# Three loads and one DMA transpose moved to other places in their queues, in a block-sparse attention with a residual MLP behind it

## The chip, the cores and the metric

The kernel runs on one core of a Trainium2 chip. The metric is the device time of one execution in microseconds (us). A core has TensorE (PE in the profile, its weight loads PEld), VectorE (DVE), ScalarE (ACT), GpSimd (POOL) and SyncE (SP). Each takes its instructions in order. Loads and stores are carried by 16 DMA engines; an instruction on POOL or SP only issues them.

## The reference

Block-sparse attention over 4 batches, 8 heads, 768 positions and 64 values per head, followed by a residual MLP with a mixing step over positions. In short:

```python
scores = (1 / sqrt(D)) * q @ k.T           # per batch and head
mask   = window | first/last block row and column | 3 sampled blocks per block row
attn   = softmax(where(mask, scores, -1e9))
x      = (attn @ v)  as [batch, seq, heads * D]       # d_model 512
a1  = alpha1 * x + beta1
tok = einsum('ts,bsd->btd', w_tok, a1)
u   = x + lam * tok
a2  = alpha2 * u + beta2
out = u + lam * (relu(a2 @ w_ch1) @ w_ch2)            # w_ch1 512 x 2048
```

## The kernel before, in words

Work goes by pairs of heads: pair i holds heads 2(i mod 4) and 2(i mod 4)+1 of batch i // 4, so there are 16 pairs, 0 to 15, four for each batch. For a pair, q, k and v are loaded with a cast to 16 bits (L322, issued on POOL), q and k are transposed, scores are computed on TensorE (L605), exponentiated on ScalarE (L623), multiplied with v on TensorE (L652 for early pairs, L675 for late ones), and normalised on VectorE (L692, L693). Behind it come the affine step (L709, L710, on POOL or VectorE), the mixing over positions (L826, L850), a cast (L869), a transpose of u (by TensorE, or by DMA on SP's queue at L902) with an affine step behind it (L893), and the two matmuls of the MLP (L923, L1075), which are woven into the attention of the next batch. Stores are issued on SP (L1088).

Two written lists set the order of the work around the change.

`PLAN` covers pairs 0 to 4, which run in 45 slots. It gives each side job a number: the whole part is the slot, the rest orders jobs within the slot (under 0.5 in the slot's early half). `loadq4` is the load of pair 4's q; `tq4`, `tk4` are pair 4's transposes on TensorE (L515), `tq5`, `tk5` those of pair 5 (L555); `lv4`, `lv5` copy v into place on VectorE (L333); `mask..` are copies on POOL (L541), `w1_..`, `w2_..` loads of the MLP's weights (L775, L781). The numbers are no times: a job runs when its engine comes to it.

`W1`, `W2`, `W2L` and `W3` cover the rest. Each row is a third of a pair, each letter a step: `d` issues one DMA transpose of u (L902), `v` the affine step on its result (L893), `g` four matmuls of the second MLP layer and after every fourth `g` a store, `K` and `Q` the DMA transposes of the next pair's k (L566) and q (L571, L574). Rows 1 and 2 of `W2L` belong to pair 12; the transposes there are those of pairs 10 and 11, the last of batch 2 counted from 0.

Buffers set what a load must wait for: q has two buffers (`qpad`), k and v have two each (`kr`, `vr`). Pair 4's loads overwrite pair 2's data, so they wait for pair 2's transposes on TensorE, and pair 5's for pair 3's.

```python
def emit_load(i, which="qkv"):                    # line 311
    ...
        nc.gpsimd.dma_start(                      # line 322
            t, src[b, 2 * hp : 2 * hp + 2].rearrange("w (p o) d -> p w (o d)", o=NT)
        )
...
def fns(s, late):                                 # line 1416
    for when, name in sorted(slots.get(s, ())):
        if (when % 1 >= 0.5) == late:
            jobs_of[name]()
```

Of the kernel before, what the change touches and what calls it, by code (L numbers as in the profile page):

```python
# [66 lines left out]
]  # L67
W2L = [
# [91 lines left out]
    "tok0_1": 16.29,  # L160
    "tok0_2": 17.09,
    "tok0_3": 18.68,
    "loadq4": 18.7,
    "lv3": 19.01,
    "loadk4": 19.19,
    "tok0_4": 19.61,
    "mask5": 20.08,
    "mask9": 20.29,
    "tq3": 20.7,
    "tok0_5": 20.76,  # L170
    "loadv5": 20.77,
    "loadq5": 21.09,
    "tk3": 22.44,
    "loadk5": 22.78,
    "udma0": 23.28,
# [1394 lines left out]
```

## Time and profile before

| | |
|---|---|
| median of 3 runs | 297.3 us (297.27 to 297.41) |
| the profiled execution | 297.57 us |
| its span, first to last instruction | 295.9 us |
| granted TensorE clock | 1.0 throughout |
| bytes moved by DMA | 31.09 MB, 105 GB/s on average |

A line of a timeline gives the start and the length of a group of like instructions in us, the engine, the line of the kernel, the operation, out<-in by the program's names, the shapes and the count; in brackets stands the idle time just before it and what ended that. A line of DMA issues gives out<-in, the issuing queue, the count, KB each (of what is written), and the us from issue to landing. In the chain of work that ended last, a line is start, length, and what.

### The profile page before, as it was taken

To read this page: it belongs to the slowest core of one execution; us is meant where nothing else is said; L and a number is where in the kernel's file an instruction comes from. 1 tells how busy PE (TensorE), PEld (TensorE's weight loads), DVE (VectorE), ACT (ScalarE), POOL (GpSimd) and SP (SyncE) were. 2 spreads that over 40 slices of the span, in tenths; PEclk is the share of its full clock that TensorE was granted. 3 is DMA by queue.
4 is the path that set the end of the run, shared out by engine and by line. 5 is a ranking of instruction groups with operands and counts; after the bars stand their busy time and mean duration, and the time that the engine had idled before them with its cause. 6 is when DMAs were issued, how large, how long until landed. Compare 5 with 4: busy or idle time off the path is not lost.

```text
span 295.9 us, 7583 instructions
## 1 busy us (share of the span) xinstructions
PE 289.2 (98%) x3097; PEld 192.7 (65%) x3097; DVE 240.6 (81%) x498; ACT 217.0 (73%) x324; POOL 110.1 (37%) x149
## 2 busy tenths in 40 slices
PE   7999999999999999999999999999999999999995
PEld 2678878665467565565576556465567678766884
DVE  4988899995668887988758788795946999999894
ACT  5999989999799872999779780899869764477000
POOL 8997978632343720347321450335320300000000
PEclk9999999999999999999999999999999999999999
DMA  6999999981392996737962957653520214400023
GB/s 176 204 198 167 193 158 204 177 143 27 95 143 60 106 190 103 109 75 98 122 122 57 142 77 161 91 123 44 96 62 2 53 38 20 151 1 3 0 91 124
DMA packets 57274, 31.09 MB, mean 105 GB/s; under 512 B 37204, under 2 KB 54016, under 8 KB 57240
## 3 DMA queue, kind: packets, MB, share of 16 engines
q0 software_dynamic: 16752, 14.22, 33.6%
q1 hardware_dynamic: 40020, 15.92, 28.2%
q8 instruction: 24, 0.39, 0.6%
q10 hardware_dynamic: 468, 0.47, 0.6%
q14 instruction: 10, 0.08, 0.1%
HBM read 29.75 MB, written 6.29 MB: 122 GB/s over the span
## 4 chain that ended last, share of the span: by engine, by line
PE 84%; DVE 5%; ACT 4%; DMA 4%; issue 1%; POOL 1%; POOLq 0%
PE mm L923 20%; PE mm L1075 16%; PE sp L605 8%; PE op L675 8%; PE mm L850 8%; PE mm L1189 5%; ACT eT L623 4%; PE mm L605 3%; DMA kr<-in_k_dram 3%; PE sp L1189 3%; PE sp L1036 3%; PE mm L1036 3%; PE op L652 2%; PE mm L826 2%; DVE eT L640 1%; DMA x_sb<-in_q_dram 1%
## 5 line engine op out<-in xcount | busy, mean ns | idle before, releaser
L623 ACT ACTIVATE eT<-sp,expb 128x1024 f16<-128x1024 f32 x111 | 118.4, 1118 | 2.4 <-PE sp L605 1.8
L640 DVE TENSOR_TENSOR eT<-eT,mask 128x1024 f16<-128x1024 f16 x99 | 80.1, 835 | 14.2 <-ACT eT L623 14.0
L709 POOL TENSOR_TENSOR a1pp<-x_sb,vbc 128x384 bf16<-128x384 f32 x25 | 28.5, 1139 | 119.2 <-DVE x_sb L693 84.6
L923 PE MATMUL mm<-uT,w1b 128*128 128x384 bf16 x384 | 70.6, 326 | 0.1
L623 ACT ACTIVATE eT<-mm,expb 128x512 f16<-128x512 f32 x66 | 41.7, 684 | 26.6 <-PE mm L605 26.3
L1075 PE MATMUL mm<-w2b,hts 128*128 128x512 bf16 x224 | 54.7, 380 | 0.0
L930 ACT ACTIVATE hts<-mm 128x384 bf16<-128x384 f32 x96 | 45.1, 501 | 10.1 <-PE mm L923 9.5
L923 PEld LDWEIGHTS <-w1b 128*128 128x128 bf16 x384 | 35.6, 98 | 23.9 <-issue 2.4
L675 PEld LDWEIGHTS <-eT 128*128 128x128 f16 x792 | 29.8, 98 | 8.5 <-issue 1.7
L1075 PEld LDWEIGHTS <-hts 128*128 128x128 bf16 x224 | 19.8, 98 | 22.3 <-issue 3.9
L675 PE MATMUL op<-vext,eT 128*128 128x65 f16 x792 | 32.2, 194 | 0.0
L605 PE MATMUL sp<-qTs,kTs 88*128 88x512 bf16 (+1 forms) x120 | 27.0, 325 | 1.3 <-ACT eT L623 0.7
L710 POOL TENSOR_TENSOR a1pp<-a1pp,vbc 128x384 bf16<-128x384 bf16 x25 | 26.9, 1075 | 2.0
L850 PE MATMUL mm<-a1pp,wtokT 128*128 128x256 bf16 x216 | 25.9, 273 | 0.1
L850 PEld LDWEIGHTS <-wtokT 128*128 128x128 bf16 x216 | 20.6, 98 | 5.6 <-issue 1.8
L1189 PEld LDWEIGHTS <-hts 128*128 128x128 bf16 x208 | 19.6, 98 | 3.3 <-issue 0.3
L862 DVE TENSOR_TENSOR x_sb<-x_sb,mm 128x512 f32<-128x512 f32 x18 | 12.3, 684 | 9.9 <-PE mm L850 9.8
L605 PE MATMUL sp<-qhT,khT 64*128 64x256 bf16 (+1 forms) x176 | 19.8, 322 | 0.0
L605 PEld LDWEIGHTS <-khT 64*128 64x128 bf16 x264 | 10.6, 94 | 12.7 <-issue 9.2
L652 PEld LDWEIGHTS <-eT 128*128 128x128 f16 x360 | 14.9, 98 | 3.8 <-issue 0.3
L1084 DVE TENSOR_TENSOR x_sb<-x_sb,mm 128x512 f32<-128x512 f32 x14 | 9.6, 685 | 8.8 <-PE mm L1075 8.7
L693 DVE TENSOR_TENSOR x_sb<-op,rcp 128x384 f32<-128x384 f32 x28 | 15.6, 557 | 1.0
(137 smaller groups left out, 395.2 us busy)
## 6 DMA issues: line engine op xcount, KB each, us to landing
out_dram<-x_sb SPq DMA_DIRECT2D x23, 256.0 KB
qpad<-in_q_dram POOLq DMA_DIRECT2D x15, 192.0 KB, 4.5
kr<-in_k_dram POOLq DMA_DIRECT2D x15, 192.0 KB, 5.3
vr<-in_v_dram POOLq DMA_DIRECT2D x15, 192.0 KB, 5.9
w1b<-in_moe_w_ch_dram POOLq DMA_DIRECT2D x4, 512.0 KB, 9.8
w2b<-in_moe_w_ch_dram POOLq DMA_DIRECT2D x4, 512.0 KB, 8.5
hts<-in_moe_w_tok_dram POOLq DMA_DIRECT2D x2, 576.0 KB, 8.9
x_sb<-in_k_dram ACTq DMA_DIRECT2D x2, 192.0 KB
```

The source lines that it names most:

```text
L605: nc.tensor.matmul(sp[jj][:, dst], lhsT, rhs, start=True, stop=True, skip_group_check=True,)
L623: nc.scalar.activation(dst, at, AF.Exp, bias=expb[:], scale=SCALE)
L640: nc.vector.tensor_mul(out=e, in0=e, in1=keep)
L652: nc.tensor.matmul(op[0][:, o, :], ets[u][:, jj, h * QB + n * P : h * QB + n * P + P], vexts[i % NVB][:, w, 2 * jp + jj, :], start=op[1] == 0,
L675: nc.tensor.matmul(op[0][:, o, :], ets[u][:, jj, h * QB + n * P : h * QB + n * P + P], vexts[i % NVB][:, w, 2 * jp + jj, :], start=op[1] == 0,
L709: eng.tensor_tensor(out=dst, in0=x_sbs[b][:, :, cols], in1=bc[0], op=ALU.mult)
L710: eng.tensor_tensor(out=dst, in0=dst, in1=bc[1], op=ALU.add)
L850: nc.tensor.matmul(ps[:, o], wtokT[:, os_, ts(2 * n + o, P)], a1pps[i][:, os_, :], start=(os_ == 0 and o == 0), stop=(os_ == NT - 1 and o ...
L923: nc.tensor.matmul(ps[:, 0:QC], w1b[:, dk, ts(n, P)], uTs[b][:, dk, ts(c, QC)], start=(dk == 0), stop=(dk == 3),)
L930: nc.scalar.activation(h_row(b, c, n), ps[:, 0:QC], AF.Relu)
L1075: nc.tensor.matmul(ps[:], ht[:, nk, ts(o % 3, P)], w2b[:, nk, :], start=(nk == 0), stop=(nk == NH - 1),)
L1189: nc.tensor.matmul(ps, a_of(b, t, a)[:, r], b_rows(m, r)[:, 0, cols], start=(start and r == ends[0]), stop=(r == ends[1]), skip_group_chec ...
```

## The change

Four edits. In `PLAN`, pair 4's q is loaded behind `tq2` (15.38), ahead of pair 4's v (15.44), and pair 4's k behind `tk2` (15.49), where both were in slots 18 and 19. Pair 5's q is loaded behind `tq3` (20.7), ahead of pair 5's v (20.77). In `W2L`, the second `d` moves from row 2, where it stood behind a `g`, to stand right behind the first in row 1.

On POOL this gives, in order of issue: the two w2b loads, q4, v4, k4, the affine step L709 and L710, two mask copies, q5, v5, k5. Before it was: the two w2b loads, v4, L709, L710, q4, k4, two mask copies, v5, q5, k5. On SP the order of two instructions changes: the second L902 now comes ahead of one store. TensorE, VectorE and ScalarE have the same instructions in the same order.

```diff
 W2L = [
     "q 0 p p g k x L x p f k 1 K 2 k",
-    "q Q 0 g x g f v v s T T x k 1 k p p g g T g g Y d 2 k",
-    "q g 0 k g d 1 2 p x k g x k",
+    "q Q 0 g x g f v v s T T x k 1 k p p g g T g g Y d d 2 k",
+    "q g 0 k g 1 2 p x k g x k",
...
-    "loadq4": 18.7,
+    "loadq4": 15.391,
     "lv3": 19.01,
-    "loadk4": 19.19,
+    "loadk4": 15.495,
...
     "loadv5": 20.77,
-    "loadq5": 21.09,
+    "loadq5": 20.705,
```

## The prediction

> **What bounds the kernel now.** I read the page first (span and busy shares), then the waits and the chain of work that ended last to find where the moved loads matter, then the timelines of the engines around that place, and last the DMA issues, asked load by load.
>
> ```profile
> span 295.9 us, 7583 instructions
> PE 289.2 (98%) x3097; PEld 192.7 (65%) x3097; DVE 240.6 (81%) x498; ACT 217.0 (73%) x324; POOL 110.1 (37%) x149
> ...
> PEld L515 <- DMA kr<-in_k_dram: 0.6, 1, 0.6
> ...
> 29.05 8.63 DMA kr<-in_k_dram
> ```
>
> TensorE is busy for 289.2 of 295.9 us, so a change can gain only where TensorE stands still or where the engine that feeds it is late. The waits name one such place for the loads that move: the transposes of pair 4's k (L515) waited once for its load. The chain has the same load in it: issued at 29.05, 8.63 us long. Here is POOL, which issues every load, around that time (start, length, engine, line, what):
>
> ```profile
> 15.28 0.76 POOL L775 DMA_DIRECT2D w1b<-in_moe_w_ch_dram  x1
> ...
> 24.07 0.72 POOL L322 DMA_DIRECT2D vr<-in_v_dram  x1
> 26.22 0.99 POOL L709 TENSOR_TENSOR a1pp<-x_sb,vbc 128x384 bf16<-128x384 f32 x1 [1.44 <-DVE x_sb L693]
> 27.29 1.06 POOL L710 TENSOR_TENSOR a1pp<-a1pp,vbc 128x384 bf16<-128x384 bf16 x1
> 28.29 0.76 POOL L322 DMA_DIRECT2D qpad<-in_q_dram  x1
> 29.05 0.72 POOL L322 DMA_DIRECT2D kr<-in_k_dram  x1
> ...
> 30.42 0.72 POOL L322 DMA_DIRECT2D vr<-in_v_dram  x1
> 31.13 0.72 POOL L322 DMA_DIRECT2D qpad<-in_q_dram  x1
> ...
> 37.39 0.99 POOL L709 TENSOR_TENSOR a1pp<-x_sb,vbc 128x384 bf16<-128x384 f32 x1 [1.00 <-DVE x_sb L693]
> ```
>
> The loads of pair 4 are v at 24.07, q at 28.29, k at 29.05; then pair 5's v at 30.42 and q at 31.13. Between v4 and q4 POOL stands 1.44 us for VectorE and then does pair 1's affine step (L709, L710). This is what the change issues q4 and k4 ahead of.
>
> When do these loads land? The issue lists of six narrow windows, one load each, give KB and us from issue to landing. In order: the first w1b block, v4, q4, k4, v5, q5.
>
> ```profile
> w1b<-in_moe_w_ch_dram POOLq DMA_DIRECT2D x1, 512.0 KB, 10.3
> vr<-in_v_dram POOLq DMA_DIRECT2D x1, 192.0 KB, 11.0
> qpad<-in_q_dram POOLq DMA_DIRECT2D x1, 192.0 KB, 7.7
> kr<-in_k_dram POOLq DMA_DIRECT2D x1, 192.0 KB, 8.6
> vr<-in_v_dram POOLq DMA_DIRECT2D x1, 192.0 KB, 8.6
> qpad<-in_q_dram POOLq DMA_DIRECT2D x1, 192.0 KB, 9.0
> ```
>
> Issue plus this time is the landing: v4 35.1, q4 36.0, k4 37.7, v5 39.0, q5 40.1. The issues of v4 and q4 lie 4.2 us apart, their landings 0.9 us. So the loads land in the order of their issue, one behind the other, about 1 us each (k4 and v5, 1.7 and 1.3), and a load spends most of its 8 to 11 us standing in the queue. The queue is not empty at any point here. This is the reading on which the forecast stands.
>
> TensorE at the two places where it takes this data, and in an undisturbed stretch for comparison:
>
> ```profile
> 22.82 0.50 PE L515 MATMUL mm<-ident,kr 128*128 128x128 bf16 x6
> ...
> 30.29 0.41 PE L652 MATMUL op<-vext,eT 128*128 128x65 f16 x8
> 30.54 0.60 PE L605 MATMUL sp<-qTs,kTs 88*128 88x512 bf16 x2
> 30.98 0.50 PE L826 MATMUL mm<-a1pp,wtokT 128*128 128x128 bf16 x6
> ...
> 36.78 0.60 PE L605 MATMUL sp<-qTs,kTs 88*128 88x256 bf16 x4
> 37.73 0.51 PE L515 MATMUL mm<-ident,kr 128*128 128x128 bf16 x6 [0.35 <-DMA kr<-in_k_dram]
> ...
> 39.34 0.60 PE L605 MATMUL sp<-qTs,kTs 88*128 88x256 bf16 x4
> 39.77 0.41 PE L652 MATMUL op<-vext,eT 128*128 128x65 f16 x8
> 40.16 0.51 PE L555 MATMUL mm<-ident,qpad 128*128 128x128 bf16 x6
> ```
>
> Four L605 matmuls are followed by the next group 0.43 us after their start (39.34 to 39.77). After 36.78 that would be 37.21, but k4's transposes start at 37.73: TensorE lost 0.52 us of issue time, of which the timeline shows 0.35 as idle. Eight L652 matmuls are followed 0.25 us later (30.29 to 30.54); after 39.77 that would be 40.02, but q5's transposes (L555) start at 40.16, right behind q5's landing at 40.1. That is a second, hidden wait of 0.14 us. ScalarE feels both:
>
> ```profile
> 39.10 2.12 ACT L623 ACTIVATE eT<-sp,expb 128x1024 f16<-128x1024 f32 x2 [0.36 <-PE sp L605]
> 41.53 10.71 ACT L623 ACTIVATE eT<-sp,expb 128x1024 f16<-128x1024 f32 x10 [0.31 <-PE sp L605]
> ```
>
> It waited 0.36 and 0.31 us for TensorE, so both engines have room to take a gain here: at most 0.52 + 0.14 = 0.66 us.
>
> **The change part by part.** *Pair 4's q and k earlier.* Nothing is added or removed; two issues on POOL move ahead of L709. The new order from 24.07 is q4 (to 24.83), v4 (to 25.56), k4 (to 26.28), then L709, which so far started at 26.22: 0.06 us later. q4 and k4 overwrite what pair 2's transposes read; those end at 22.82 + 0.50 = 23.3, so POOL does not stand for them. The wait list of the built program lets k4's issue also wait for the load eight issues ahead, which is the w1b block: landed at 15.28 + 10.3 = 25.6, when POOL comes to k4 anyway. L709 and L710 are on no tight path: they end at 28.4, and the first matmul on pair 1's result is L826 at 30.98, 2.6 us later. What POOL does behind them (masks, pair 5's loads) comes 1.4 us earlier, until it again waits for VectorE at 37.39. Cost on POOL: 0.
>
> On the queue: before, k4 stands behind v4 and q4; after, behind q4 and v4, the same bytes. With a queue that is never empty, q4 takes v4's landing (35.1), v4 takes q4's (36.0) and k4 keeps 37.7. k4's transposes come ahead of q4's on TensorE, so q4's earlier landing helps nobody. Gain: 0. The bounds: a gain of the whole 0.52 us, if k4 lands by 37.2; a loss of 1.3 us, if it slips to the next place in the queue, v5's 39.0. I take 0, since order and distance of the landings, not the issue times, fit all five rows.
>
> The Trainium skill (DMA: Bandwidth & Descriptors, Anatomy of one DMA) fits a load issued on this path as about 2.0 us plus its bytes over 436 GB/s; for 192 KB that is an estimate of 2.5 us, by which k4 would land at 28.0 and the 0.52 us would be gained. The trace disagrees for loads in a queue, with 8.6 us.
>
> *Pair 5's q ahead of its v.* They change places: q5 takes 39.0, v5 takes 40.1. The hidden wait of 0.14 us goes, since q5 is there a whole microsecond before 40.02. The next thing that could be late is v5, copied by VectorE (L333):
>
> ```profile
> 42.43 0.37 DVE L333 COPY vext<-vr 128x768 f16<-128x768 f16 x1
> ```
>
> That is 2.3 us after the new landing: covered. Gain: 0.14 us, bounds 0 (if ScalarE takes it back) and 0.14.
>
> *The two transposes by DMA together.* On SP's queue the second L902 moves ahead of one store (L1088):
>
> ```profile
> 184.28 1.21 SPq L902 DMA_TRANSPOSE uraw<-ubf  x1
> 188.27 0.33 SPq L1088 DMA_DIRECT2D out_dram<-x_sb  x1
> 188.65 2.40 SPq L902 DMA_TRANSPOSE uraw<-ubf  x1
> 191.16 1.23 SPq L571 DMA_TRANSPOSE qhT<-qpad  x1
> ...
> 192.94 0.48 DVE L893 TENSOR_SCALAR uT<-uraw,ab2T 128x768 bf16<-128x768 bf16 x1 [0.28 <-DMA uraw<-ubf]
> ...
> 194.00 1.46 PE L923 MATMUL mm<-uT,w1b 128*128 128x384 bf16 x8
> ```
>
> Now it can start at 184.28 + 1.21 = 185.5, and even with the 2.40 us of its old place it ends at 187.9, before the store's 188.27. The store is not delayed; the transposes behind it (L571) may come up to 2.4 us earlier, which nobody needs. VectorE stood 0.28 us for this transpose, at the second L893. That wait goes. But the L893 ends at 193.42, and the first matmul that reads it starts at 194.00 behind other matmuls: 0.58 us of cover. Gain: 0, bounds 0 and 0.28.
>
> **Sum.** 0 + 0.14 + 0 = 0.14 us less. The profiled execution took 297.57 us (its span and 1.7 us around it) and would take 297.43. It lies 0.27 above the median of 297.3, so on the median's scale the time is 297.16, given as 297.2. About 0.2% (0.6 us) is what a measurement of this kernel can tell from no change; the forecast is inside.
>
> **The rivals.**
>
> *Earlier issue is earlier landing.* If the queue does have gaps that the narrow windows hide, k4 lands before 37.2, its wait goes with q5's: 0.66 us, and 296.6; with half of k4's wait 0.4 us, and 296.9. For it speaks that k4's issue moves 3.5 us ahead and that this wait is on the chain; by the skill's rule above this would be the outcome. Against it stand the landings, 0.9 us apart for issues 4.2 us apart.
>
> *k4 lands later.* After the change pair 4's and 5's loads queue up 1.4 us sooner, while a DMA transpose runs beside them. Two loads of equal size took 1.7 and 1.3 us here instead of 0.9, so something already takes turns with them. The skill (same page, Queues, rings and completion order) says that each DMA engine goes round between the queues that have work, packet by packet; the longer steps agree with it. If the heavier stretch falls wholly on what precedes k4, every microsecond is paid by TensorE at 37.73, one for one, up to v5's old place: 1.3 us, and 298.6; half of it is 297.95. It decides from a slip of 0.75 us on, since 0.14 is gained elsewhere. Against it: the bytes ahead of k4, and the transpose's own start, do not change.
>
> *The reorder does nothing at all*, q5's 0.14 us being taken back by ScalarE: 297.3, inside the forecast's verdict.
>
> **How the numbers follow.** Forecast with the third rival 0.52: no change. Earlier landing 0.24, of which 0.18 passes 0.2% (nearly all of k4's wait gained) and 0.06 does not. Later landing 0.20, all counted as slower. For what I don't see 0.04, half each way, since two parts shift work on POOL and SP under engines that are nearly full. So faster 0.20, same 0.58, slower 0.22. The range runs from the first rival's 296.6 to half of the second's price, 297.9; beyond lie half of the second rival and the unseen, 0.14.
>
> **What would show it.** Right: k4's issue near 25.6 with some 12 us to landing, k4's transposes still near 37.7 with an idle of about 0.35; q5's L555 about 0.25 us behind its L652; the 0.28 us before L893 gone and L923 no earlier against the matmuls around it. Wrong: no idle before L515 (first rival), or k4's landing after 38 (second). A time outside 296.7 to 297.9 with these rows as forecast would mean that a shift on POOL or SP, costed here at nothing, has a price.

## The result

The changed kernel takes 296.65 us (median of 22 runs), the kernel before 297.38 (22 runs beside it): 0.73 us less, a ratio of 0.9978 with a 95% interval of 0.9969 to 0.9986. (Differences in us are of medians, here and below; the ratios are not ratios of medians, so the two need not agree.) That is inside the range on record. But it is five times the forecast's 0.14 us, and as the experiments show, its parts are not those of the forecast.

The first profiled execution of the changed kernel was the longest of its 22, at 298.55 us. First lines of its page:

```profile
span 296.8 us, 7585 instructions
...
PE 290.5 (98%) x3097; PEld 193.1 (65%) x3097; DVE 240.9 (81%) x498; ACT 217.0 (73%) x324; POOL 109.5 (37%) x149
```

and a row of its waits:

```profile
DVE w2b L787 <- DMA w2b<-in_moe_w_ch_dram: 2.0, 1, 2.0
```

VectorE stood 2.0 us at L787, which reads a weight load that took 11.4 us from issue to landing in this execution; the other profiles of either kernel do not have this wait. In the same execution k4 landed at 38.0 us, and L515 started 0.25 us late for it. A second profile of each kernel (296.84 us for the changed one, 297.32 for the one before) is compared here. First the changed kernel at the places that the prediction showed, POOL's timeline:

```profile
24.51 0.72 POOL L322 DMA_DIRECT2D qpad<-in_q_dram  x1
25.20 0.74 POOL L322 DMA_DIRECT2D vr<-in_v_dram  x1
25.91 0.75 POOL L322 DMA_DIRECT2D kr<-in_k_dram  x1
26.69 1.01 POOL L709 TENSOR_TENSOR a1pp<-x_sb,vbc 128x384 bf16<-128x384 f32 x1
...
29.64 0.77 POOL L322 DMA_DIRECT2D qpad<-in_q_dram  x1
```

and TensorE's:

```profile
37.24 0.60 PE L605 MATMUL sp<-qTs,kTs 88*128 88x256 bf16 x4
37.67 0.50 PE L515 MATMUL mm<-ident,kr 128*128 128x128 bf16 x6
...
39.71 0.41 PE L652 MATMUL op<-vext,eT 128*128 128x65 f16 x8
39.96 0.50 PE L555 MATMUL mm<-ident,qpad 128*128 128x128 bf16 x6
```

The issues moved as expected, and neither transpose group waits: L515 comes 0.43 us behind L605, L555 0.25 behind L652. But TensorE's rows in the second profile of the kernel before show no wait either:

```profile
36.79 0.60 PE L605 MATMUL sp<-qTs,kTs 88*128 88x256 bf16 x4
37.22 0.50 PE L515 MATMUL mm<-ident,kr 128*128 128x128 bf16 x6
...
39.26 0.41 PE L652 MATMUL op<-vext,eT 128*128 128x65 f16 x8
39.51 0.50 PE L555 MATMUL mm<-ident,qpad 128*128 128x128 bf16 x6
```

In that profile k4 was issued at 28.94. From issue to landing it took, by the issue list of a narrow window,

```profile
kr<-in_k_dram POOLq DMA_DIRECT2D x1, 192.0 KB, 6.7
```

and in the changed kernel's

```profile
kr<-in_k_dram POOLq DMA_DIRECT2D x1, 192.0 KB, 10.5
```

k4 landed at 35.6 here, against 37.7 in the first profile of the same kernel, and at 36.4 with the change, though it was issued 3 us earlier. TensorE wants it at 37.2 to 37.7. So the wait on which the prediction was worked out belonged to one execution, not to every execution of the kernel.

What does differ between the two kernels lies near 193 us, near 271 us and at the end. VectorE near 193 us in the kernel before:

```profile
191.53 0.47 DVE L893 TENSOR_SCALAR uT<-uraw,ab2T 128x768 bf16<-128x768 bf16 x1
192.63 0.48 DVE L893 TENSOR_SCALAR uT<-uraw,ab2T 128x768 bf16<-128x768 bf16 x1 [0.63 <-DMA uraw<-ubf]
193.03 1.28 DVE L640 TENSOR_TENSOR eT<-eT,mask 128x1024 f16<-128x1024 f16 x2
194.23 0.19 DVE L692 RECIPROCAL rcp<-op 128x6 f32<-128x6 f32 x1
194.45 0.56 DVE L693 TENSOR_TENSOR x_sb<-op,rcp 128x384 f32<-128x384 f32 x1
```

TensorE beside it:

```profile
193.33 1.46 PE L923 MATMUL mm<-uT,w1b 128*128 128x384 bf16 x8
195.06 0.91 PE L675 MATMUL op<-vext,eT 128*128 128x65 f16 x24 [0.27 <-DVE x_sb L693]
```

The changed kernel issues both transposes in one stretch on SP:

```profile
184.07 2.54 SPq L902 DMA_TRANSPOSE uraw<-ubf  x2
```

The second has landed at 188.2 there, where it landed at 192.6 before. The changed kernel's VectorE:

```profile
191.98 0.86 DVE L893 TENSOR_SCALAR uT<-uraw,ab2T 128x768 bf16<-128x768 bf16 x2
...
194.18 0.56 DVE L693 TENSOR_TENSOR x_sb<-op,rcp 128x384 f32<-128x384 f32 x1
```

and its TensorE:

```profile
193.79 1.46 PE L923 MATMUL mm<-uT,w1b 128*128 128x384 bf16 x8
195.09 0.90 PE L675 MATMUL op<-vext,eT 128*128 128x65 f16 x24
```

Before, VectorE stands 0.63 us in front of the second L893. It takes its instructions in order, so the L693 behind it, which empties the accumulator that TensorE's next L675 writes, comes late, and L675 starts 1.73 us behind L923 instead of 1.30: 0.43 us lost. With both transposes issued at 184 us, the two L893 run back to back and the loss is gone.

A smaller difference lies near 271 us, on ScalarE and TensorE's weight loads in the kernel before:

```profile
270.02 1.09 ACT L1011 COPY part<-sp 128x384 f32<-128x384 f32 x2
...
271.17 0.10 PEld L1036 LDWEIGHTS <-wsum 128*128 128x128 bf16 x1 [0.15 <-issue]
```

In the changed kernel these two copies take 0.86 us and the weight load does not stand. The stand ("issue": for nothing that the profile shows) is there in all six profiles of kernels with the transposes apart and in none of the seven with them together. From L675 at 195 us to the end of the last VectorE instruction it is 97.3 us in the six and 97.2 in the seven, 0.09 us less. With the transposes together, the trace has one wait instruction fewer on ScalarE (at L869) and one more on SP (at L902). That the missing wait is what shortens ScalarE's copies was not tested by itself.

At the end, the last VectorE instruction of the kernel before (first profile, whose span is 295.9 us):

```profile
292.38 0.29 DVE L1199 TENSOR_TENSOR x_sb<-x_sb,op 128x128 f32<-128x128 f32 x1 [0.16 <-PE op L1189]
```

and of the changed kernel (second profile):

```profile
292.01 0.29 DVE L1199 TENSOR_TENSOR x_sb<-x_sb,op 128x128 f32<-128x128 f32 x1 [0.16 <-PE op L1189]
```

with the first line of its page:

```profile
span 295.1 us, 7566 instructions
```

From the last computation to the end of the span it is 295.9 - 292.67 = 3.2 us before and 295.1 - 292.30 = 2.8 us after: nearly 0.4 us. The experiments trace it to POOL's program being longer by two instructions. (The totals of two profiles can also differ by 19, by matmul records that are missing from some of them.)

### The profile page after: what moved, and what is told of

Its sections match the earlier page's. It is cut to its first block, busy times and chain, and to the rows that moved or that the text cites. A ratio compares the mean times of both kernels' runs of the same rounds, so it can differ in the third digit from the quotient of the medians.

```text
span 296.8 us, 7585 instructions
## 1 busy us (share of the span) xinstructions
PE 290.5 (98%) x3097; PEld 193.1 (65%) x3097; DVE 240.9 (81%) x498; ACT 217.0 (73%) x324; POOL 109.5 (37%) x149
## 3 DMA queue, kind: packets, MB, share of 16 engines
q0 software_dynamic: 16752, 14.22, 36.4%
## 4 chain that ended last, share of the span: by engine, by line
PE 83%; DVE 6%; DMA 5%; ACT 3%; POOL 1%; issue 1%; DVEq 0%
PE mm L923 20%; PE mm L1075 16%; PE sp L605 8%; PE op L675 8%; PE mm L850 8%; PE mm L1189 5%; DMA w2b<-in_moe_w_ch_dram 4%; PE mm L605 3%; PE sp L1189 3%; PE mm L1036 3%; PE sp L1036 3%; ACT eT L623 2%; PE op L652 1%; DVE eT L640 1%; DMA x_sb<-in_q_dram 1%; PE op L1189 1%
## 5 line engine op out<-in xcount | busy, mean ns | idle before, releaser
L640 DVE TENSOR_TENSOR eT<-eT,mask 128x1024 f16<-128x1024 f16 x99 | 80.4, 839 | 13.9 <-ACT eT L623 13.7
L709 POOL TENSOR_TENSOR a1pp<-x_sb,vbc 128x384 bf16<-128x384 f32 x25 | 28.5, 1139 | 120.2 <-DVE x_sb L693 84.9
L923 PE MATMUL mm<-uT,w1b 128*128 128x384 bf16 x384 | 70.6, 326 | 0.1
L923 PEld LDWEIGHTS <-w1b 128*128 128x128 bf16 x384 | 35.6, 98 | 23.9 <-issue 2.4
L675 PEld LDWEIGHTS <-eT 128*128 128x128 f16 x792 | 29.9, 98 | 8.3 <-issue 1.7
L675 PE MATMUL op<-vext,eT 128*128 128x65 f16 x792 | 32.1, 194 | 0.0
L605 PE MATMUL sp<-qTs,kTs 88*128 88x512 bf16 (+1 forms) x120 | 27.0, 326 | 1.0 <-ACT eT L623 0.7
L710 POOL TENSOR_TENSOR a1pp<-a1pp,vbc 128x384 bf16<-128x384 bf16 x25 | 26.7, 1069 | 2.0
L605 PE MATMUL sp<-qhT,khT 64*128 64x256 bf16 (+1 forms) x176 | 19.8, 322 | 0.0
L605 PEld LDWEIGHTS <-khT 64*128 64x128 bf16 x264 | 10.6, 94 | 12.7 <-issue 9.2
L652 PEld LDWEIGHTS <-eT 128*128 128x128 f16 x360 | 14.9, 98 | 4.6 <-issue 1.2
L693 DVE TENSOR_TENSOR x_sb<-op,rcp 128x384 f32<-128x384 f32 x28 | 15.6, 558 | 1.0
```

Source lines behind the costliest of these rows:

```text
L605: nc.tensor.matmul(sp[jj][:, dst], lhsT, rhs, start=True, stop=True, skip_group_check=True,)
L640: nc.vector.tensor_mul(out=e, in0=e, in1=keep)
L652: nc.tensor.matmul(op[0][:, o, :], ets[u][:, jj, h * QB + n * P : h * QB + n * P + P], vexts[i % NVB][:, w, 2 * jp + jj, :], start=op[1] == 0,
L675: nc.tensor.matmul(op[0][:, o, :], ets[u][:, jj, h * QB + n * P : h * QB + n * P + P], vexts[i % NVB][:, w, 2 * jp + jj, :], start=op[1] == 0,
L709: eng.tensor_tensor(out=dst, in0=x_sbs[b][:, :, cols], in1=bc[0], op=ALU.mult)
L710: eng.tensor_tensor(out=dst, in0=dst, in1=bc[1], op=ALU.add)
```

## The experiments

Four theories were tested. *Queue theory*, the prediction's: loads land in the order of their issue, so moving q4 and k4 changes nothing and q5's move gains its hidden wait. *Gap theory*, its first rival: earlier issue, earlier landing. *Theory A*: the DMA transpose's wait at L893, through VectorE's order. *Theory C*, which came from the traces of the first eight experiments: two instructions more on POOL move a fetch of its program away from the end of the kernel.

**One part at a time.** First the two transposes alone (the change's two rows of `W2L`, `PLAN` as before):

> Only the two u transposes together, all loads as before. Queue theory (loads land in the order of their issue, so only pair 5's q gains) and gap theory (the queue has gaps, so an earlier issue is an earlier landing): both 0 us, within 0.1 of before. A third theory, that the SP reorder is what gained: 0.4 to 0.7 us less than before.

Measured: 296.90 us (296.71 to 296.97) beside 297.31 for before, ratio 0.9979 (0.9969 to 0.9989). The part that the prediction costed at nothing gains 0.41 us, and the spread of the runs, 296.74 to 298.61 for before, shrinks to a quarter of a us. (By the ratio it would be 0.6 us.)

Pair 5's q alone:

```diff
-    "loadq5": 21.09,
+    "loadq5": 20.705,
```

> Only pair 5's q ahead of its v. Queue theory: 0.14 us less than before, L555 directly behind L652 (0.25 us after its start). Gap theory: the same 0.14. If this gives 0.4 us or more, q5's hidden wait is mostly longer than in the one trace of before.

Measured: 296.91 us, ratio 0.9985 (0.9975 to 0.9994). It gains 0.40 us, more than any wait for q5 that a profile of before shows. That looked like a longer hidden wait, and was not.

Pair 4's q and k alone (15.391 and 15.495, the rest as before):

> Only pair 4's q and k early. Queue theory: 0 us, k4 lands where it did (37.7 in the trace of before, give or take the start), and L515 still waits 0.3 to 0.5 us. Gap theory: k4 lands before TensorE comes to it, L515 waits for nothing, 0.4 to 0.55 us less than before.

Measured: 297.48 us, ratio 1.0009 (0.9987 to 1.0031): nothing, as the queue theory had it. But the wait at L515 that this theory expected was not there, as it was not in before's second profile, so the time does not tell the two theories apart. The landing does: k4 was issued at 25.57, 3 us earlier than before, and landed at 35.3, inside the spread of its landings in the old order, 35.1 to 37.7 in nine profiles. The profile shows how far the other wait can go, on VectorE:

```profile
193.21 0.48 DVE L893 TENSOR_SCALAR uT<-uraw,ab2T 128x768 bf16<-128x768 bf16 x1 [0.79 <-DMA uraw<-ubf]
```

and on TensorE:

```profile
193.75 1.46 PE L923 MATMUL mm<-uT,w1b 128*128 128x384 bf16 x8
195.64 0.91 PE L675 MATMUL op<-vext,eT 128*128 128x65 f16 x24 [0.43 <-DVE x_sb L693]
```

VectorE stands 0.79 us, and L675 starts 1.89 us behind L923: 0.59 lost. In the first profile of before it was 0.28 us, and 1.37 behind: 0.07 lost. With a stand of 0.40 (`q5_only`) and 0.45 us (`before_pad`) it lost 0.19 and 0.26. So TensorE loses what exceeds 0.2 us, 0.31 us on the mean of these five profiles, and how much that is changes from execution to execution.

The change with k4 first of pair 4's three loads:

```diff
-    "loadv4": 15.44,
-    "loadq4": 15.391,
-    "loadk4": 15.495,
+    "loadv4": 15.498,
+    "loadq4": 15.495,
+    "loadk4": 15.491,
```

> The change, and pair 4's k issued first of the three loads of pair 4 (k4, q4, v4 in place of q4, v4, k4). Queue theory: k4 takes the first of the three places, near 35, two us earlier, so its wait of 0.5 us goes on top of the change: 0.4 to 0.5 us less than with the change alone. Gap theory: the wait is gone already with the change, so the same time as the change, within 0.15 us.

Measured: 296.60 us, ratio 0.9975 (0.9965 to 0.9985), as with the change. k4 landed at 34.8 (issued at 24.19, 10.6 us later), the place near 35 that the queue theory gave it; the gain that it added to this did not come, because the changed kernel has no such wait to lose in a usual execution.

**Is it VectorE's order?** The second profile of the kernel before:

> The kernel before, looked at once more, to see which of its waits come back. Theory A (the load waits of the first profile were that run's landing times, the DMA transpose's wait is what is always there): no idle before L515, L555 right behind its L652, and VectorE waits again for the second u transpose at L893, 0.3 to 0.8 us, of which TensorE loses what exceeds 0.2 at the L675 behind it. Rival (the load waits are always there): L515 waits about 0.5 us again.

Its rows stand in the result: theory A on both points. Then the stand was filled with work, leaving SP and the DMA transposes alone. Of the kernel before, one `v` in row 3 of `W2L` moves behind the next `k`, which puts one L640 ahead of the second L893:

```diff
-    "q 0 p k x v Q v 1 2 p k x g k g",
+    "q 0 p k x v Q 1 2 p k v x g k g",
```

> The kernel before with the second L893 one VectorE instruction later (behind one of the two L640 that followed it); loads and DMA transposes untouched. Theory A (VectorE stands in order for the transpose, so the L640, L692 and L693 behind it come late and TensorE waits at L675): the stand is filled with 0.6 us of work, and most of what the two transposes together gain comes without moving them: 0.3 to 0.45 us less than before, and a spread as narrow as theirs. Rival (what gains is on SP's queue or in the DMA engines, not on VectorE): 0 us.

Measured: 297.00 us (296.75 to 297.23), ratio 0.9989 (0.9981 to 0.9998): 0.32 us less, three quarters of what the moved transposes gain. The runs spread over 0.5 us, nearly twice as wide as theirs. VectorE, then TensorE:

```profile
192.28 0.68 DVE L640 TENSOR_TENSOR eT<-eT,mask 128x1024 f16<-128x1024 f16 x1
192.89 0.47 DVE L893 TENSOR_SCALAR uT<-uraw,ab2T 128x768 bf16<-128x768 bf16 x1
```

```profile
193.70 1.46 PE L923 MATMUL mm<-uT,w1b 128*128 128x384 bf16 x8
195.00 0.90 PE L675 MATMUL op<-vext,eT 128*128 128x65 f16 x24
```

No wait at L893, and L675 is back at 1.30 us behind L923. The transpose is as late as ever: issued at 188.36, it landed at 192.74, 4.4 us later, against 4.3 and 4.6 in the two profiles of before. So the gain at L675 comes from VectorE's order. The missing 0.09 us is the stand near 271 us, which this kernel still has (0.15 us at L1036) and the moved transposes do not.

**What does q5's place pay?** Transposes together and q5 ahead of v5, without pair 4's loads:

> The two transposes together, and pair 5's q ahead of its v; pair 4's loads as before. Theory A (the runs of the transposes alone have no load wait left in most executions): 296.9 to 296.7, so 0 to 0.2 less than the transposes alone. Rival (q5's wait is worth 0.4 us in every run, as the run of it alone suggests): 296.5.

Measured: 296.59 us (296.55 to 296.75), ratio 0.9975 (0.9966 to 0.9984). This is as low as the whole change and as steady as any kernel here; pair 4's loads add nothing to it. It is 0.31 us below the transposes alone, though neither profile has a wait for q5. Theory A, which had 296.7 to 296.9 here, does not explain this. (The 95% intervals of the two ratios overlap; differences of 0.3 us between these kernels rest on the medians and on what the traces show.)

The other way: transposes together, q5 behind k5.

```diff
-    "loadq5": 21.09,
+    "loadq5": 22.785,
```

> The two transposes together, and pair 5's q behind its k, so one place later in the queue than before, two later than with the change. Queue theory: it lands some 1.1 us later than before, 40.7 to 41.2; L555 wants it at 39.8 to 40.0, so TensorE waits 0.8 to 1.2 us and the time is 0.7 to 1.2 above that of the transposes alone (297.6 to 298.1). Gap theory: the issue is 0.7 us later, the landing too, so 0.3 to 0.6 us.

Measured: 297.82 us, ratio to before 1.0014 (1.0003 to 1.0025), 0.92 above the transposes alone. q5 was issued at 32.24, took 9.0 us and landed at 41.2. TensorE:

```profile
39.74 0.41 PE L652 MATMUL op<-vext,eT 128*128 128x65 f16 x8
41.25 0.51 PE L555 MATMUL mm<-ident,qpad 128*128 128x128 bf16 x6 [1.09 <-DMA qpad<-in_q_dram]
```

That is the queue theory with its price: one place in the queue is a microsecond, and where the slack is used up TensorE pays it. With the load order of before q5 is just inside its slack: in the profile of the transposes alone it landed at 39.6, 0.2 us ahead of L555. Moving it earlier had nothing to gain there.

**The end of the kernel.** All profiles of kernels with q5 ahead of v5 had 2.8 us behind the last VectorE instruction and one or two POOL instructions more in the trace; all others had 3.2. These instructions are waits in front of loads (L322): with q5 ahead of v5, one wait for two earlier loads becomes two waits for one each, and one further wait stands ahead of pair 6's loads. The queue that the page calls "instruction" (q14) moves 8 KB at a time; the kernels with the longer end have such a packet in their last microseconds, the others do not. So the transposes alone, with two idle instructions added behind POOL's last work:

```diff
+    for _ in range(2):
+        nc.gpsimd.memset(gate[:], 0.0)
```

> The two transposes together, loads as before, and two tiny memsets (128x1) at the end of POOL's program, where POOL is idle for 60 us: they add no work to any path. Theory C (the kernels with pair 5's q ahead of its v have two POOL instructions more, by which POOL's last code fetch moves from the end of the kernel to an idle stretch, and the end is 0.35 us shorter): 2.8 us from the last VectorE instruction to the end of the span in place of 3.2, no 8 KB instruction packet at the end, and a median 0.35 us below that of the transposes alone (296.9), 296.5 to 296.6. Rival (q5's earlier landing is what pays): 296.9, with the tail at 3.2 or the gain not there.

Measured: 296.60 us, ratio 0.9978 (0.9966 to 0.9990), 0.30 below the transposes alone and equal to `dd_q5`. The last VectorE instruction of the transposes alone, whose span is 295.3 us:

```profile
291.80 0.29 DVE L1199 TENSOR_TENSOR x_sb<-x_sb,op 128x128 f32<-128x128 f32 x1 [0.16 <-PE op L1189]
```

the instruction queue in a window over its last microseconds (packets, MB, share):

```profile
q14 instruction: 1, 0.01, 0.4%
```

and the padded kernel, whose span is 294.7 us and whose same window has no such row:

```profile
291.58 0.29 DVE L1199 TENSOR_TENSOR x_sb<-x_sb,op 128x128 f32<-128x128 f32 x1 [0.16 <-PE op L1189]
```

That is 3.2 and 2.8 us. The semaphore instructions in the packed traces, which the views leave out, show where the time goes. At the very end POOL waits for SP and then signals the other engines: between these two instructions it takes 0.36 us in the transposes alone and 0.07 in the padded kernel, and the same (0.36 to 0.38 against 0.07) in all profiles with the longer and the shorter end. The 8 KB packet starts 0.7 to 1.0 us after that stand has ended, so it is not what POOL stands for. In `k4_first`, with one POOL instruction more, it comes at 234.9, 1.0 us after the instruction ahead of POOL's wait.

The changed kernel again, with the rows in the result:

> The changed kernel once more, since its first profile was 1.9 us above its median. Theory: no wait on the w2b block at L787 (that was this run's landing), L515 and L555 without a wait, the two L893 back to back, the tail 2.8 us: 296.5 to 296.8.

The rows came out as expected; the time, 296.84 us, is just above what was expected. And the padding on the kernel before:

> The kernel before with the same two tiny memsets at the end of POOL's program and nothing else. Theory C (the end of the kernel and the u transposes are two separate gains that add up): 0.35 us below before, 296.9 to 297.05, tail 2.8 us, and the wait at the second L893 still there with its spread (296.4 to 298). Rival (the padding helps only together with the moved transposes, or not at all): 297.2 to 297.4.

Measured: 296.93 us (296.40 to 297.73) beside 297.22, ratio 0.9984 (0.9970 to 0.9997): 0.29 less, with a wait of 0.45 us at the second L893 still there, a spread of over a microsecond, and the tail at 2.8 us. Two instructions that do nothing gain 0.3 us; this gain and that of the transposes are separate.

Together, from medians: transposes 0.41 (VectorE's order 0.32, the stand near 271 us 0.09), two more POOL instructions 0.29 to 0.30, sum 0.70 to 0.71; the change gains 0.73.

## Why the prediction was right or wrong

The range held the time, by luck: 296.65 us lies 0.05 inside its lower end, which came from a rival that did not happen, and what gained was costed at nothing or stood in no term of the sum. The likeliest case, no change, did not come clearly out: 0.73 us is just beyond the bound of 0.6, with an interval (0.14% to 0.31%) that reaches to both sides of it. The rival that gave nearly this number, earlier landing at 296.6, was wrong in its reason. The prediction's last sign pointed the right way, though the rows at L515 were not as forecast: a time below 296.7 was to mean that a shift on POOL or SP has a price.

*Pair 4's loads, 0.* Right in the sum, and right about the queue: k4 keeps its place behind the same bytes, a place is about a microsecond (k4 first, q5 behind k5). Wrong in what it took for given: the 0.52 us before L515. It was one execution's landing, 37.7; in the eight other profiles with k4 in the same place (`before_again`, `dd_only` and `v_late` among them) nothing waited. The 0.14 us for q5 failed on the same step. A term read off one execution was taken as present in all.

*The fit and the second rival.* The Trainium skill's fit of about 2 us plus bytes (DMA: Bandwidth & Descriptors, Anatomy of one DMA) fails in this queue: k4 took 6.2 to 11.7 us. The second rival, a later k4, did not come on the median; the changed kernel's first profile has some of it, with k4 at 38.0.

*Pair 5's q, 0.14.* The number was wrong and so was the reason; it pays 0.3 to 0.4 us at the end of the kernel, by program length on POOL. The prediction held that nothing is added or removed. In the traces the change has two waits more on POOL, one more on SP and one fewer on ScalarE: an edit which leaves the engines' work alone changes the number of wait instructions. The tail of 3.2 us is in no term of the sum.

*The transposes, 0.* This is the mis-sized term: 0.41, of which 0.32 at L675. The working found the stand of VectorE and asked who reads the result of L893 (L923, 0.58 us later). It should have asked what stands behind L893 on VectorE: L640, L692, L693, and with them TensorE's L675. That cover is 0.2 us, and the stand itself was among the smallest seen, 0.28 against 0.40 to 0.79 in the four other profiles with the transposes apart and `v` in its old place. Its own bound, 0 to 0.28, was also one execution's. The 0.09 us near 271 us lies outside everything that this term considered.

*POOL, 0.* Right on the median: L709 starts at 26.69 and nothing behind it is late in the second profile. The wait of k4's issue for the w1b block, which the prediction put at nothing, was 0.54 us in the changed kernel's first profile.

What stays open: what POOL stands for at the end, since that a fetch of its program is at work is inferred from where the 8 KB packets fall; whether ScalarE's missing wait works in the same way near 271 us; and what makes the start of the kernel and the landing times differ by 0.5 to 2 us between executions of one program.

## What to carry to other kernels

A wait in one profile is one draw: before pricing it, take a second profile, or at least see how much slack its landing had in the queue. When an engine that works in order stands for a late input, the cover to count is that of everything queued behind the standing instruction, not of the reader of its result. And when a change alters only an order of issues, compare the instruction counts too: waits are instructions, and program length alone moved this kernel by 0.3 us.

## What the runs showed of the hardware

The loads on POOL's queue landed strictly in the order of issue in every profile, pair 4's three loads of 192 KB 0.8 to 1.7 us apart, with the same load's landing 2 us apart between two executions of one program (k4 at 35.6 and 37.7). Two idle POOL instructions shortened the end of the kernel from 3.2 to 2.8 us: POOL's step from its last wait for SP to its signal took 0.07 us in place of 0.36, and one 8 KB instruction packet was gone from the last microseconds. An order of DMA issues changed the number of wait instructions on three engines.
